# Relu-squared attention and MLP on one core: first keys in two loads, a split copy of q^T, and stores of two row positions in one

## The chip, the cores and the metric

The kernel runs on one core of one Trainium2 chip. The metric is device time in microseconds (us). The kernel before was run three times: 369.5, 369.84 and 369.86 us, a median of 369.84.

The engines are named as in the profile: PE is TensorE's matmul, PEld its weight load, DVE is VectorE, ACT is ScalarE, POOL is GpSimd and SP is SyncE. SPq, ACTq and POOLq are the queues on which these engines issue DMAs.

## What is computed

```
scores = q @ k^T / 8                     # q, k, v: 8 batches, 12 heads, 448 positions, 64 wide, float32
attn   = max(scores, 0)^2 / 448
o      = attn @ v
x      = o, heads side by side           # 3584 x 768
h      = x @ w_in                        # 768 x 2048
out    = (max(h, 0)^2) @ w_out           # 2048 x 768, out is 3584 x 768 float32
```

There is no softmax, so a score tile can be squared and used as soon as it exists.

## The kernel before

**Units and tiles.** A unit is four heads of one batch (`NU = 3` units for each of 8 batches, 24 in all). The 448 positions of a head are written as `(p j)`: 64 values of `p` and `J = 7` of `j`, so position = 7 p + j, and one partition holds 7 neighbouring positions. A unit gives 7 score tiles. Each tile is computed by `score` as 64x64 products into a PSUM slot, goes through a ReLU on ACT (line 273) into a 128x896 tile `at`, and is squared on DVE (`square0`, line 304, in the first batch; line 388 later). Then `av0` or `av_unit` multiplies it with v. There are two PSUM slots in rotation (`slot`), and a third one in the first batch (`third`).

**The head.** Units 0 to 5 are loaded as fp16 (`load16`, lines 91 to 96, POOL queue) and transposed on TensorE; units from 6 on are transposed by DMA on SP (`dma_transpose`, line 120). The order of the first batch is written out by hand in lines 804 to 898. Ten warm-up products (`warm`) run first. Then `turn_first` (lines 203 to 217) transposes q and then k of unit 0: 14 small transposes each, a copy out of PSUM, a warm-up product. DVE copies q^T whole; of k^T, ACT copies the first of 7 blocks and DVE the other six. Then come scores 0 to 3 and `pe_transpose(1)`, which turns q and k of unit 1 in one PSUM slot, with two copies on DVE (line 229). `pe_transpose(2)` comes after score 8. Argument 2 of `score`, the default of the helper `s`, runs the same products twice, which keeps TensorE busy; scores 0, 4 and 9 are run once.

**The later stages.** Two batches make a pair, pr = 0 to 3. A pair's hidden layer (line 430 for the first pair, 559 for the others) is followed by its output products (line 746), with the scores and attention products of later batches between them (`visit`).

**Output products and stores.** A row tile `(pr, tb)` is 128 rows of the pair's 896: partitions 0 to 63 are position j of one batch, 64 to 127 position j + 1, or the first position of the next batch where tb is 3. `o_groups` takes two row tiles at a time and forms seven products (`products`, lines 713 to 720) instead of eight, in two accumulators X and Y. Pairs 0 and 2 have three groups, pairs 1 and 3 have four (with row tile 6 of the pair before). The results go to `osb[0]` and `osb[1]`, 128x768 float32, of which there are two buffers each (`late["osb"]`, line 924). `end2` makes the first write of osb[0] (line 653), right after product 2; product 4 in program order (k = 3) starts afresh in the same Y. `end4` stores osb[1], `end3` stores osb[0]. A store is two DMAs on SP, one for each half of 64 partitions:

```python
b, j = divmod(2 * tb + i, J)          # i = 0, 1: the halves
out[b*S:(b+1)*S, :].rearrange("(p j) d -> p j d", j=J)[:, j, c]  <-  osb[64*i : 64*i+64, c]
```

The last group (`LAST`) stores in parts as they come: osb[0]'s first half and osb[1]'s second half on SP, osb[1]'s first half on POOL, and the rest of osb[0] in two quarters, each with one half on SP and the other on ACT.

SP's queue holds the DMA transposes and the stores in one order. Each of the 16 counters for DMAs (8 for the queues of SP and ACT, 8 for POOL) is used in rotation, so a DMA also waits for the one eight places before it.

Of the kernel before, what the change touches and what calls it, by code (L numbers as in the profile page):

```python
# [11 lines left out]
FP16 = mybir.dt.float16  # L12
FP32 = mybir.dt.float32
AF = mybir.ActivationFunctionType
# [4 lines left out]
def kernel(  # L19
# [9 lines left out]
    nc = tc.nc  # L29

    B, H, S, D = q.shape
# [11 lines left out]
    P = 128  # L43
    J = 7
# [36 lines left out]
    def heads(t, n):  # L81
        b, u = divmod(n, NU)
        return t[b].rearrange(
            "(hh u hp) (p j) d -> u (hp p) hh (j d)", hh=2, hp=2, j=J)[u]
# [6 lines left out]
    def load16(n):  # L91
        tq = q16_p.tile([P, 2, J * D], FP16, name="q16", tag="q16")
        tk = q16_p.tile([P, 2, J * D], FP16, name="k16", tag="k16")
        nc.gpsimd.dma_start(out=tq, in_=heads(q, n))
        nc.gpsimd.dma_start(out=tk, in_=heads(k, n))
        q16s[n] = (tq, tk)

    def load_v(n):
        t = v_p.tile([P, 2, J * D], FP16, name="vt", tag="vt")
        nc.gpsimd.dma_start(out=t, in_=heads(v, n))  # L100
        vts[n] = t
# [12 lines left out]
    def new_qkt():  # L114
        return [qkt_p.tile([P, J, P], FP16, name=nm, tag=nm) for nm in ("qT", "kT")]
# [30 lines left out]
    def sums_w2(i):  # L146
# [5 lines left out]
        nc.vector.tensor_sub(dst[:, c], x[:, c], y[:, c])  # L152

    load16(0)
    ident = const_p.tile([P, P], FP16, name="ident", tag="ident")
    make_identity(nc, ident)
# [37 lines left out]
    def slot(dtype, third=False):  # L194
        return (third_p if third else s_p).tile(
            [P, 2, 2048 // mybir.dt.size(dtype)], dtype, name="slot", tag="slot")

    def warm(ps, n):
        for _ in range(n):
            nc.tensor.matmul(ps[:, 0, 0:S], lhsT=zeros[:, 0:P], rhs=zeros,  # L200
                             start=True, stop=True)

    def turn_first(ps):

        ts = new_qkt()
        for i, src in enumerate(q16s.pop(0)):
            tps = slot(FP16)[:, i, 0:J * P].rearrange("p (j c) -> p j c", j=J)
            for j in range(J):
                for hh in range(2):
                    nc.tensor.transpose(  # L210
                        tps[64 * hh:64 * hh + 64, j],
                        src[:, hh, j * D:(j + 1) * D], ident)
            if i:
                nc.scalar.activation(out=ts[i][:, 0], in_=tps[:, 0], func=AF.Copy)
            nc.vector.tensor_copy(ts[i][:, i:J], tps[:, i:J])
            warm(ps, 1)
        qkt[0] = ts

    def pe_transpose(n):
        srcs = q16s.pop(n)  # L220
        ts = new_qkt()
        ps = None if n > 3 else slot(FP16)

        def copy(i, act=False):
            dst, ps = ts[i].rearrange("p j c -> p (j c)"), pss[i][:, i if n < 4 else 0, 0:J * P]
            if act:
                nc.scalar.activation(out=dst, in_=ps, func=AF.Copy)
            else:
                nc.vector.tensor_copy(dst, ps)

        if n > 3:
            pss = [mm_tile(None, FP16).rearrange("p (i c) -> p i c", i=1) for _ in range(2)]
        else:
            pss = [ps, ps]
        for i, src in enumerate(srcs):
            for j in range(J):
                for hh in range(2):
                    nc.tensor.transpose(  # L238
                        pss[i][64 * hh:64 * hh + 64, i if n < 4 else 0, j * P:(j + 1) * P],
                        src[:, hh, j * D:(j + 1) * D], ident)  # L240
        qkt[n] = ts
        if n == 3:
            return lambda: copy(0, True), lambda: copy(1)
        copy(0, n > 3)
        copy(1)
# [8 lines left out]
    def score(t, times=1, third=False, ps=None):  # L254
        n, j = divmod(t, J)
        qT, kT = qkt[n]
        spare = ps is not None
        ps = slot(FP32, third) if ps is None else [mm_tile(ps), mm_tile(ps)]
        for hh in list(range(2)) * times:
            r = slice(64 * hh, 64 * hh + 64)  # L260
            for hp in range(2):
                c = slice(64 * hp, 64 * hp + 64)
                nc.tensor.matmul(  # L263
                    ps[hh][c, 0:S] if spare else ps[c, hh, 0:S],
                    lhsT=kT[r, j, c], rhs=qT[r, :, c],
                    start=True, stop=True)
        at = at_p.tile([P, 2, S], FP16, name="at", tag="at")
        if spare:
            for hh in range(2):
                nc.scalar.activation(  # L270
                    out=at[:, hh], in_=ps[hh][:, 0:S], func=AF.Relu, scale=SK)
        else:
            nc.scalar.activation(out=at, in_=ps[:, :, 0:S], func=AF.Relu, scale=SK)  # L273
        ats[t] = at
        seen[t] = now[0]

    def av0(*tiles):

        for t in tiles:
            n, j = divmod(t, J)  # L280
            vt, at = vts[n], ats.pop(t)
            if j == 0:
                avt[0] = [p.tile([P, 512], FP32, name="avt", tag="av") for p in av_ps]
            for hp in range(2):
                r = slice(64 * hp, 64 * hp + 64)
                for hh in range(2):
                    nc.tensor.matmul(  # L287
                        avt[0][hp][64 * hh:64 * hh + 64, 0:S],
                        lhsT=vt[r, hh, j * D:(j + 1) * D], rhs=at[r, hh, :],
                        start=(j == 0), stop=(j == J - 1))  # L290
# [11 lines left out]
    def square0(*tiles):  # L302
        for t in tiles:
            nc.vector.tensor_mul(ats[t], ats[t], ats[t])  # L304
# [3 lines left out]
    def av_due(more=0):  # L308
        n = unit[0]
        return n < NUN and seen.get(n * J + J - 1, 10 ** 6) < now[0] + more  # L310
# [263 lines left out]
        return [(0.096, step(p, r, m), r == 0 and m == 0 and p not in (0, 1, 6, 8))  # L574
                for p in range(14) for r in range(2) for m in range(NH)]

    def store(row, osb, c, eng, eng2=None):
        pr, tb = row
        for i in range(2):
            b, j = divmod(2 * tb + i, J)  # L580
            b += 2 * pr
            (eng2 if eng2 and i else eng).dma_start(  # L582
                out=out[b * S:(b + 1) * S, :].rearrange(
                    "(p j) d -> p j d", j=J)[:, j, c],
                in_=osb[64 * i:64 * i + 64, c])
# [31 lines left out]
    def o_groups(groups, then):  # L617
# [5 lines left out]
        def group(n, rows, last):  # L623
# [3 lines left out]
            c0, c1 = slice(0, HALF), slice(HALF, DM)  # L627
# [8 lines left out]
            def ahead(i, k=n):  # L636
                if k < len(groups) and i not in sets[k]:
                    flush_g(needs(k))
                    sums(i, groups[k], sets[k])
# [11 lines left out]
            def plus(row, c, nm, acc=Y, cc=slice(0, HALF)):  # L651
                now_ve(0.5)
                nc.vector.scalar_tensor_tensor(  # L653
                    out=osb[row][:, c], in0=acc[0][:, 0:cc.stop - cc.start], scalar=CO,
                    in1=keep[nm][:, cc], op0=ALU.mult, op1=ALU.add)
# [8 lines left out]
            def end2():  # L664
                new_osb()
                plus(0, c0, "m1")
                if last:
                    store(rows[0], osb[0], c0, nc.sync)
# [22 lines left out]
            def end4():  # L691
                if last:
                    plus(1, c0, "u3", acc=Z)
                    store(rows[1], osb[1], c0, nc.gpsimd)
                    return
                nc.scalar.activation(out=osb[1][:, c0], in_=X[0][:, 0:HALF],
                                     func=AF.Copy, scale=CO)
                store(rows[1], osb[1], slice(0, DM), nc.sync)
                ahead(1, n + 1)
                ahead(2, n + 1)  # L700
# [5 lines left out]
            def end3_part(z):  # L706
                h = HALF // 2
                cc = slice(z * h, z * h + h)
                c = slice(HALF + cc.start, HALF + cc.stop)
                plus(0, c, "u5", acc=W, cc=cc)  # L710
                store(rows[0], osb[0], c, nc.sync, nc.scalar)

            products = (
                (X, True, lambda: tile_of(rows[0])[:, LO], b11, end1),
# [87 lines left out]
    NB0 = NU * J  # L802
    ps = slot(FP32, True)
    warm(ps, 10)
    turn_first(ps)

    def s(t, times=2):
        score(t, times, third=t in THIRD)

    THIRD = (0, 3, 5, 8, 10, 13, 16, 19)  # L810
    s(0, 1)
    s(1)
    s(2)
    s(3)
    square0(0, 1)
    pe_transpose(1)
    load16(3)
    load_w1(0)
    load_w1(1)
    load_v(3)  # L820
    s(4, 1)
    s(5)
    square0(2)
    av0(0, 1)
    s(6)
# [3 lines left out]
    square0(4)  # L829
    s(8)  # L830
    av0(3)
    square0(5, 6)
    pe_transpose(2)
    load16(4)
    load_w1(2)
    load_v(4)
    s(9, 1)
    square0(7)
    s(10)
    av0(4, 5)  # L840
    square0(8)
    s(11)
# [149 lines left out]
    for cost, fn, edge in steps:  # L992
        while ev and edge and ev[0][0] <= clock + 1e-3:
            ev.popleft()[1]()
        if edge and clock >= plan[0][0]:
# [6 lines left out]
            elif pair is not None and ahead <= 1.5 and clock > last + 1.25:  # L1002
                n = min(pair[1 + av_due(1)], NT - tile_no)
# [3 lines left out]
            elif ahead <= (1.5 if soon else 0.0) and clock > last + 1.5:  # L1007
                n = min(2, NT - tile_no)
# [38 lines left out]
```

## Time and profile before

One execution was profiled. It took 369.71 us; the profile's span is 367.9 us, and the 1.8 us left lie around it.

| stretch | us from the span's start | what ends it |
|---|---|---|
| warm-up, loads of q and k | 0 to 7.36 | k of unit 0 landed, turned and copied |
| first batch's scores | 7.36 to 27.6 | ReLU on ACT, squares and copies on DVE |
| everything up to the last products | 27.6 to 362.7 | TensorE |
| last writes and stores | 362.7 to 366.3 | landing of the last store |

The most important rows of the page, beside those shown in the prediction, are the costliest groups. L273 (ReLU) is 135.5 us of ACT, L388 (squares) 86.7 us of DVE, L746 and L559 are TensorE's output and hidden products. Idle time of an engine other than TensorE costs nothing as such. L653, the first write of an output buffer, is 30 instructions of 541 ns.

In the profile's rows, `[idle before <-releaser]` says how long the engine stood idle before the instruction and whose end let it go. The median of 52 stores of 192 KB is 3.3 us from issue to landing.

### The profile page before, as it was taken

Reading aid. Unit: us, or ns where it says so; the run is one execution under the profiler, and the core shown is the slowest. Engines: PE = TensorE matmul, PEld = TensorE weight load, DVE = VectorE, ACT = ScalarE, POOL = GpSimd, SP = SyncE. Lnnn points to the kernel's source line nnn. Section 1 sums busy time; section 2 is a strip of 40 time slices with the busy share of each in tenths; the row PEclk is TensorE's granted clock in tenths of the full one; section 3 lists DMA queues with packets and bytes.
Section 4 is the critical chain, followed back from the end, with each engine's and each line's share of the span. In section 5 each row is a group of like instructions: output and inputs, shape, how many; then the busy total and the mean of one; then the engine's idle time right before and its main releaser. Section 6 shows DMA issues by size and latency. Waiting matters only on the chain.

```text
span 367.9 us, 8740 instructions
## 1 busy us (share of the span) xinstructions
PE 358.8 (98%) x3588; PEld 232.1 (63%) x3588; DVE 265.3 (72%) x470; ACT 248.6 (68%) x384; POOL 107.2 (29%) x128
## 2 busy tenths in 40 slices
PE   8899999999999999999999999999999999999994
PEld 3644445445556788875555687886555689976662
DVE  2997677987867679888575667788876687784442
ACT  3988895788676998877655678886766785532220
POOL 8635521856552254531045225320000000000001
PEclk9999999999999999999999999999999999999999
DMA  8999999999999999967799998992323300003333
GB/s 119 196 204 203 205 204 161 144 160 166 207 124 155 170 111 134 99 92 61 138 146 125 156 159 83 107 90 52 67 71 87 86 3 2 2 0 87 86 96 78
DMA packets 121160, 42.65 MB, mean 116 GB/s; under 512 B 100832, under 2 KB 117760, under 8 KB 121120
## 3 DMA queue, kind: packets, MB, share of 16 engines
q0 software_dynamic: 82912, 23.01, 61.7%
q1 hardware_dynamic: 38048, 18.98, 26.5%
q8 instruction: 28, 0.46, 0.5%
q10 hardware_dynamic: 160, 0.10, 0.1%
q14 instruction: 12, 0.10, 0.1%
HBM read 45.61 MB, written 11.01 MB: 154 GB/s over the span
## 4 chain that ended last, share of the span: by engine, by line
PE 89%; DVE 4%; ACT 3%; issue 2%; DMA 1%; POOL 0%; POOLq 0%; ACTq 0%
PE mm L746 33%; PE mm L559 27%; PE mm L430 9%; PE slot L263 9%; PE slot L329 7%; ACT at L273 2%; DVE at L388 1%; DMA k<-in_k_dram 1%; DVE at L304 1%; PE mm L263 1%; PE avt L287 1%; PE slot L238 1%; ACT xt L342 1%; PE mm L238 0%; DVE osb L653 0%
## 5 line engine op out<-in xcount | busy, mean ns | idle before, releaser
L273 ACT ACTIVATE at<-slot 128x896 f16<-128x896 f32 x156 | 135.5, 927 | 7.4 <-PE slot L263 7.4
L388 DVE TENSOR_TENSOR at<-at 128x896 f16<-128x896 f16 x147 | 86.7, 618 | 12.6 <-ACT at L273 11.9
L109 POOL DMA_DIRECT2D qs<-in_q_dram x36 | 35.3, 983 | 111.1 <-DMA qT<-qs 102.8
L746 PEld LDWEIGHTS <-s 128*128 128x128 f16 x440 | 41.8, 98 | 32.2 <-issue 4.8
L559 PEld LDWEIGHTS <-w 128*128 128x128 f16 x576 | 53.8, 98 | 6.8 <-issue 6.0
L263 PE MATMUL slot<-qT,kT 64*64 64x448 f16 x696 | 53.2, 359 | 1.9 <-ACT at L273 1.4
L559 PE MATMUL mm<-xt,w 128*128 128x224 f16 x432 | 49.2, 259 | 0.0
L746 PEld LDWEIGHTS <-g 128*128 128x128 f16 x336 | 31.9, 98 | 23.5 <-issue 3.8
L559 PEld LDWEIGHTS <-ws 128*128 128x128 f16 x432 | 40.8, 98 | 2.8 <-issue 2.8
L746 PE MATMUL mm<-b,g 128*128 128x384 f16 x224 | 40.7, 326 | 0.0
L430 PE MATMUL mm<-xt,w 128*128 128x448 f16 x192 | 39.8, 354 | 0.0
L746 PE MATMUL mm<-b,s 128*128 128x384 f16 x216 | 39.5, 326 | 0.0
L746 PE MATMUL mm<-t,s 128*128 128x384 f16 x224 | 38.8, 326 | 0.0
L109 POOL DMA_DIRECT2D ks<-in_k_dram x36 | 35.2, 979 | 9.6 <-DMA b<-in_moe_w_out_dram 5.8
L263 PEld LDWEIGHTS <-kT 64*64 64x64 f16 x744 | 20.3, 104 | 27.6 <-issue 21.5
L653 DVE SCALAR_TENSOR_TENSOR osb<-mm,u 128x384 f32<-128x384 f32 (+1 forms) x30 | 16.2, 541 | 28.4 <-ACT u L648 20.9
L582 POOL DMA_DIRECT2D out_dram<-osb x2 | 1.1, 563 | 120.9 <-DVE osb L653 120.9
L502 DVE CUSTOM_DVE_ANT_0 g<-mm,m 128x448 f16<-128x448 f32 x36 | 22.4, 621 | 18.4 <-PE mm L559 7.8
L648 ACT ACTIVATE u<-mm 128x384 f32<-128x384 f32 x28 | 14.2, 507 | 30.5 <-PE mm L746 28.4
L559 PE MATMUL mm<-x,ws 128*128 128x224 f16 x288 | 33.7, 259 | 0.0
L329 PE MATMUL slot<-at,vt 64*64 64x448 f16 x560 | 30.1, 349 | 0.0
L430 PEld LDWEIGHTS <-w 128*128 128x128 f16 x192 | 17.1, 98 | 19.2 <-issue 5.1
(80 smaller groups left out, 417.2 us busy)
## 6 DMA issues: line engine op xcount, KB each, us to landing
out_dram<-osb SPq DMA_DIRECT2D x52, 192.0 KB, 3.3
vt<-in_v_dram POOLq DMA_DIRECT2D x24, 224.0 KB, 6.8
qs<-in_q_dram POOLq DMA_DIRECT2D x36, 112.0 KB, 4.9
ks<-in_k_dram POOLq DMA_DIRECT2D x36, 112.0 KB, 5.8
w<-in_moe_w_in_dram POOLq DMA_DIRECT2D x8, 384.0 KB, 12.1
b<-in_moe_w_out_dram POOLq DMA_DIRECT2D x4, 768.0 KB, 17.1
q<-in_q_dram POOLq DMA_DIRECT2D x6, 224.0 KB, 7.2
k<-in_k_dram POOLq DMA_DIRECT2D x6, 224.0 KB, 7.7
```

Of the source, the lines that this page charges most:

```text
L109: nc.gpsimd.dma_start(out=t[:, :, hh, :], in_=heads(src, n)[:, hh].rearrange("p (j d) -> p j d", d=D))
L238: nc.tensor.transpose(pss[i][64 * hh:64 * hh + 64, i if n < 4 else 0, j * P:(j + 1) * P], src[:, hh, j * D:(j + 1) * D], ident)
L263: nc.tensor.matmul(ps[hh][c, 0:S] if spare else ps[c, hh, 0:S], lhsT=kT[r, j, c], rhs=qT[r, :, c], start=True, stop=True)
L273: nc.scalar.activation(out=at, in_=ps[:, :, 0:S], func=AF.Relu, scale=SK)
L329: nc.tensor.matmul(ps[hp][64 * hh:64 * hh + 64, 0:S] if spare else ps[64 * hh:64 * hh + 64, hp, 0:S], lhsT=vt[r, hh, j * D:(j + 1) * D], r ...
L388: lambda: nc.vector.tensor_mul(at, at, at), 0))
L430: nc.tensor.matmul(cell[0][:, 0:S], lhsT=w1[f // 4][:, m, (f % 4) * P:(f % 4 + 1) * P], rhs=xts[b][:, m, :], start=(m == 0), stop=(m == NM ...
L502: nc.vector._custom_dve(TENSOR_ADD_SAT, out=gs(s, hi, right), in0=acc(s, y), in1=keep[s, nm], s0=3.4e38, s1=0.0)
L559: nc.tensor.matmul(XY[s][y][:, r * Q:(r + 1) * Q], lhsT=left(k, i0 + 2 * s + r, m), rhs=right(k, m), start=(fresh and r == 0 and m == 0), ...
L648: nc.scalar.activation(out=t, in_=X[0][:, 0:HALF], func=AF.Copy, scale=CO)
L653: nc.vector.scalar_tensor_tensor(out=osb[row][:, c], in0=acc[0][:, 0:cc.stop - cc.start], scalar=CO, in1=keep[nm][:, cc], op0=ALU.mult, op ...
L746: nc.tensor.matmul(acc[0][:, 0:HALF], lhsT=left()[:, f], rhs=right[:, f], start=(fresh and f == 0), stop=(f == KH - 1), skip_group_check=n ...
```

## The change

It does four things.

1. k of unit 0 is loaded in two DMAs, j = 0 to 3 and j = 4 to 6.
2. `turn_first` copies q^T with DVE (blocks 0 to 3) and ACT (4 to 6), transposes the first four blocks of k, copies block 0 and then 1 to 3 on DVE, runs score 0, and only then transposes and copies the other three blocks. q and k get a PSUM slot each, and one warm-up product of two is left out.
3. Scores 4 and 9 are placed ahead of `pe_transpose(1)` and `pe_transpose(2)`. Of the scores around them 4, 5 and 10 are run once, and 9 twice.
4. `store` writes both halves of a row tile in one DMA where both lie in the same batch (tb other than 3). In the last group osb[1]'s first half goes to ACT's queue instead of POOL's, and the two quarters go whole to ACT and to SP.

```diff
@@ load16
-        nc.gpsimd.dma_start(out=tk, in_=heads(k, n))
+        for js in (slice(0, 4), slice(4, J)) if n == 0 else (slice(0, J),):
+            c = slice(js.start * D, js.stop * D)
+            nc.gpsimd.dma_start(out=tk[:, :, c], in_=heads(k, n)[:, :, c])
@@ turn_first
-    def turn_first(ps):
-        ts = new_qkt()
-        for i, src in enumerate(q16s.pop(0)):
-            tps = slot(FP16)[:, i, 0:J * P].rearrange("p (j c) -> p j c", j=J)
-            for j in range(J):
+    def turn_first(first_score):
+        qT, kT = new_qkt()
+        qkt[0] = qT, kT
+        tq, tk = q16s.pop(0)
+        qp, kp = [slot(FP16)[:, 0, 0:J * P].rearrange("p (j c) -> p j c", j=J)
+                  for _ in range(2)]
+        def turn(dst, src, js):
+            for j in js:
                 for hh in range(2):
                     nc.tensor.transpose(
-                        tps[64 * hh:64 * hh + 64, j],
+                        dst[64 * hh:64 * hh + 64, j],
                         src[:, hh, j * D:(j + 1) * D], ident)
-            if i:
-                nc.scalar.activation(out=ts[i][:, 0], in_=tps[:, 0], func=AF.Copy)
-            nc.vector.tensor_copy(ts[i][:, i:J], tps[:, i:J])
-            warm(ps, 1)
-        qkt[0] = ts
+        turn(qp, tq, range(J))
+        nc.vector.tensor_copy(qT[:, 0:4], qp[:, 0:4])
+        nc.scalar.activation(out=qT[:, 4:J], in_=qp[:, 4:J], func=AF.Copy)
+        turn(kp, tk, range(4))
+        nc.vector.tensor_copy(kT[:, 0:1], kp[:, 0:1])
+        nc.vector.tensor_copy(kT[:, 1:4], kp[:, 1:4])
+        warm(ps, 1)
+        first_score()
+        turn(kp, tk, range(4, J))
+        nc.vector.tensor_copy(kT[:, 4:J], kp[:, 4:J])
@@ store
-    def store(row, osb, c, eng, eng2=None):
+    def store(row, osb, c, eng):
         pr, tb = row
+        b, j = divmod(2 * tb, J)
+        if j + 1 < J:
+            b += 2 * pr
+            eng.dma_start(
+                out=out[b * S:(b + 1) * S, :].rearrange(
+                    "(p j) d -> j p d", j=J)[j:j + 2, :, c],
+                in_=osb[:, c])
+            return
         for i in range(2):
             b, j = divmod(2 * tb + i, J)
             b += 2 * pr
-            (eng2 if eng2 and i else eng).dma_start(
+            eng.dma_start(
@@ end4, end3_part (last group)
-                    store(rows[1], osb[1], c0, nc.gpsimd)
+                    store(rows[1], osb[1], c0, nc.scalar)
-                store(rows[0], osb[0], c, nc.sync, nc.scalar)
+                store(rows[0], osb[0], c, (nc.scalar, nc.sync)[z])
@@ the first batch, by hand
-    turn_first(ps)
-    s(0, 1)
+    turn_first(lambda: s(0, 1))
     s(1)
     s(2)
     s(3)
+    s(4, 1)
     square0(0, 1)
     pe_transpose(1)
...
-    s(4, 1)
-    s(5)
+    s(5, 1)
...
     av0(3)
+    s(9)
     square0(5, 6)
     pe_transpose(2)
...
-    s(9, 1)
     square0(7)
-    s(10)
+    s(10, 1)
```

## The prediction

> **What bounds the kernel now.** I read the page first (busy shares, slices, the chain that ended last), then the list of DMA issues, then busy time by stage, then the timeline at the head and in the last output stage.
>
> ```profile
> span 367.9 us, 8740 instructions
> ...
> PE 358.8 (98%) x3588; PEld 232.1 (63%) x3588; DVE 265.3 (72%) x470; ACT 248.6 (68%) x384; POOL 107.2 (29%) x128
> ...
> PE   8899999999999999999999999999999999999994
> ...
> PE 89%; DVE 4%; ACT 3%; issue 2%; DMA 1%; POOL 0%; POOLq 0%; ACTq 0%
> ...
> out_dram<-osb SPq DMA_DIRECT2D x52, 192.0 KB, 3.3
> ```
>
> TensorE carries 89% of the chain and is busy in every slice but the first two and the last. So whatever delays TensorE in the middle is paid in full, and a gain can only come from the head (about 8 us) or the tail (about 5 us). Nothing in the chain is a store: each lands 3.3 us after its issue (median), far ahead of its next use.
>
> ```profile
> 93.00:120.00 27.00, 27.00 (x247) 14.88 (x246) 20.59 (x37) 18.34 (x30) 11.03 (x13) 1.00 1.27 160
> 166.00:213.00 47.00, 47.00 (x407) 26.33 (x406) 32.50 (x57) 29.07 (x48) 13.90 (x16) 1.00 0.95 128
> 257.00:293.00 36.00, 36.00 (x328) 20.52 (x327) 25.82 (x47) 24.55 (x40) 0.00 (x0) 1.00 0.31 78
> 329.00:364.00 35.00, 33.73 (x216) 20.63 (x214) 16.43 (x30) 6.87 (x14) 1.12 (x2) 1.00 0.30 82
> ```
>
> These are the stretches with stores of the four output stages (O0 to O3): window, length, PE, PEld, DVE, ACT, POOL, clock, DMA share, GB/s. PE is full in the first three. The DMA engines are crowded in O0 and O1 (the share is a sum of overlapping packet times, so it passes 1) and nearly free in O2 and O3.
>
> ```profile
> 335.96 2.48 SPq L582 DMA_DIRECT2D out_dram<-osb  x4
> 336.75 0.56 DVE L653 SCALAR_TENSOR_TENSOR osb<-mm,u 128x384 f32<-128x384 f32 x1 [1.50 <-PE mm L746]
> ...
> 345.06 2.48 SPq L582 DMA_DIRECT2D out_dram<-osb  x4
> ...
> 347.20 0.56 DVE L653 SCALAR_TENSOR_TENSOR osb<-mm,m 128x384 f32<-128x384 f32 x1 [0.80 <-PE mm L746]
> ```
>
> A group of two row tiles (9.1 us here) stores its osb1 and then, 1.4 us later, its osb0, in four issues. There are two buffers of each. So L653 at 347.20, the first write of osb0 in the third group, needs the store of the first group's osb0, issued at 337.33. It has 9.9 us; the store takes 2.8.
>
> **What the Trainium skill says.** (1) "DMA: Bandwidth & Descriptors", section "Why a DMA increments its semaphore by 16 and not by 1": a DMA runs on k of the 16 engines, k being the largest number up to 16 that divides the slowest dimension (above 1) of both access patterns; on the SP and ACT queues it takes the lowest-numbered k. (2) The same page, "Queues, rings and completion order": SP and ACT have one ring each on the same 16 engines, and each engine takes a ring in order. (3) "TensorE: Matmul & The Clock Gate", "What's actually happening": after an idle window of about 3.4 us the clock is halved until about 3.4 us of work have passed. The trace before has k = 16 only (64 rows on both sides; 16 landings for each store), so it neither supports nor contradicts (1); it agrees with (3) at the start, where full clock is granted 4.5 us after the first matmul.
>
> **The merged stores.** In the built program the DRAM side of a merged store is 2 x 64 x 768, the pair of row positions j outermost, and the SBUF side is 128 x 1 x 768. By (1) k = 2: engines 0 and 1 carry every merged store, 64 rows each, where 4 rows per engine and issue went before. 24 of the 28 row tiles are merged (not position 3, whose two halves lie in different batches). Issues fall from 62 to 35, which saves SP time that bounds nothing.
>
> Price: the trace's packet records show 121 ns for a 3072-byte packet in quiet stretches, 65 for 1536, 36 for 768. So 64 of them take S = 7.7, 4.2 and 2.3 us on one engine. Shorter is possible: packets overlap by some 16 ns in the loads (768-byte packets of 79 ns pass one in 60), and the skill's fabric ceiling (same page, "Where 436 GB/s comes from") gives an estimate of 27.2 GB/s an engine, 113 ns; with 105 ns S is 6.7. Longer is possible where loads share the engine. I take 121. The first packet comes 1.1 us after the issue, the landing 0.4 after the last packet (packet records of 361 and 359).
>
> Who waits: L653 stands on DVE and holds the sums and squares behind it. TensorE's product 3 starts afresh in the accumulator Y that this L653 reads, so TensorE follows about 0.5 us later. I write need = L653's time + 0.5.
>
> - O3 (no loads). Both engines work without a gap from 337.1: groups 1 and 2 four stores (30.8), group 3 one merged (7.7) and one unmerged (8 rows each, 1.0), the last group three half rows (12.6) and two quarters (4.6): 56.7. Last packet 393.8, landing 394.2, against 366.3 now: +27.9. On the way L653 waits: group 1's osb0 lands at 337.1 + 15.4 + 0.4 = 352.9, need 347.7; group 2's at 368.3, need 356.8 + 5.2 = 362.0. These 11.5 us lie inside the 27.9, since the engines never run dry.
> - O2. Stores of the first group at 264.93 and 267.42 land by 266.0 + 15.4 + 0.4 = 281.8; need 280.93 + 0.5: +0.5.
> - O1. First group at 175.16 and 176.81: 176.3 + 15.4 + 0.4 = 192.1, need 189.37 + 0.5: +2.2. The second group's wait behind them and behind two transposes of the same ring (1.0 each, 256-byte packets): 191.7 + 2.0 + 15.4 = 209.1, and one unit's loads lie in it (four of 0.9 and one of 1.2, the pace at which such loads land in a line: 4.8): 213.9 + 0.4. Need 201.29 + 0.5 + 2.2 = 204.0: +10.3. Together 12.5.
> - O0. Stores at 93.71 and 95.78: 94.8 + 15.4 + 0.4 = 110.6, with a unit's loads 115.4; need 108.95 + 0.5. Between 1 and 6, up to 10 if the transposes behind (97.26) come late for their scores; I take 5.
> - Cold clock: the stalls of O0 and O1 pass 3.4 us; half of 3.4 is lost in each, 3.4. The slower TensorE also gives the stores time: I take 2. In O3 it hides beneath the stores.
>
> **The head.** q landed at 5.28 and k at 6.37 (landing records), so 4/7 of k lands near 5.9. Eight transposes (14 take 0.58), then a DVE copy of 512 columns and one of 128 (625 ns for 896 and 558 for 768 give about 0.43 and 0.23; ACT's half of q^T is done by 6.6): the first score can start at 6.75 instead of 7.36. The second load adds an issue of 0.7 us on POOL in front of the identity (3.45, then 4.2; needed at 5.3) and of every later load, but the loads queue on the engines anyway (q of unit 1 is issued at 3.40 and lands at 7.90); two smaller packets cost about 0.1 us. k's rest lands at about 6.5, before the score is out of TensorE.
>
> ```profile
> 7.80 17.18 ACT L273 ACTIVATE at<-slot 128x896 f16<-128x896 f32 x21 [0.49 <-PE slot L263]
> ...
> 10.59 0.63 DVE L229 COPY qT<-slot 128x896 f16<-128x896 f16 x1 [0.40 <-PE slot L238]
> ...
> 26.40 0.62 DVE L299 TENSOR_SCALAR xt<-avt 128x448 f16<-128x448 f32 x1 [0.76 <-PE avt L287]
> 26.94 0.61 DVE L229 COPY kT<-slot 128x896 f16<-128x896 f16 x1
> 27.61 0.14 PEld L263 LDWEIGHTS <-kT 64*64 64x64 f16 x8 [0.49 <-DVE kT L229]
> ```
>
> ACT's 21 ReLUs run without a gap and move up by 0.6. DVE does not: it is nearly full from 10.59 to 25.64 (27 instructions at 0.535), and the transposes, one score later, now wait for the third ReLU (about 9.7) where they waited for the second (9.57). Its copies come 0.15 later. What is left is the 0.7 us in which DVE waited at 26.40: 0.3 of it goes. Bounds -0.6 (all that ACT gains) and +0.2 (the copies' delay); I take -0.3. The warm-up products left out (one, and one set of score 5) cover nothing that TensorE waits for.
>
> **Sum.** 27.9 + 0.5 + 12.5 + 5 + 2 - 0.3 = 47.6. The profiled execution took 369.7 (span 367.9 and 1.8 around it), 0.1 below the median: 417.3, forecast 417.
>
> **The rivals.**
> - Two engines, but only the end pays: stores are a little faster (105 ns a packet), loads yield, and O0 to O2 hide them behind the two buffers. For it: O2 is within 0.5 us of hiding already. Against it: O1's second group misses by 10. 369.7 + 27.9 - 0.3 = 397, down to 389 with faster packets.
> - Two engines, another pair each time: stores run beside one another. Group 1's osb0 in O3 lands at 337.33 + 1.1 + 7.7 + 0.4 = 346.5, before its need; the last half row on ACT at 362.25 + 1.1 + 4.2 + 0.4 = 368.0, +1.7: 371. Against it: the skill's lowest-numbered k.
> - Not slower: the store is spread over all 16 engines after all, because dimensions are reordered on the way to the queue. Its place is the tail: two issues of POOL and four quarter stores become two, the last quarter lands near 363.15 + 2.1 (the smallest landing time shown) + 0.3 instead of 366.3, about -0.7, and with the head -0.3: 368.7. It decides as soon as k is 8 or more: S is then at most 1.9 us and no buffer is late. Against it: nothing in the built program shows a reordering.
>
> **Chances.** Forecast's mechanism in all stages 0.72, with its own range 398 (105 ns) to 440 (loads and transposes late too). Only the end 0.12 (388 to 398), changing pair 0.05 (371), sixteen engines 0.11 (368.7). 0.2% is 0.74 us, about what a measurement of this kernel can tell from no change. Of the last case 0.07 is faster by more, 0.04 within; all others are slower. The range 388 to 445 takes in the first two cases but for their edges, about 0.8.
>
> **What would show it.** Right: stores that land 10 to 20 us after issue; L653 (L675 after) waiting for DMA out_dram in O1 and O3; PE gaps there; SP's landings as the end of the chain, with TensorE done some 15 us earlier; in the head, the first score near 6.8. Wrong: stores landing in 3 us, or a span below 375, would say that k is not 2 on fixed engines; a first score after 7.2, that half of k does not land early.

## The result and the profile after

| | before | after |
|---|---|---|
| device time, median | 369.85 us (4 runs, 369.5 to 370.1) | 439.44 us (4 runs, 437.47 to 441.23) |
| span of the profiled execution | 367.9 us | 435.9 us |
| mean granted TensorE clock | 0.999 | 0.937 |

The change makes the kernel slower by 19%: the ratio is 1.188, with a 95% interval of 1.181 to 1.195. The forecast was 417, with a range of 388 to 445. The four runs of the changed kernel lie in two pairs, at 437.5 to 437.7 and at 441.2, so two or three us between single runs of kernels like it decide nothing.

In the code after, L653 has become L675, L746 is L768, L559 is L572, L263 is L276; L596 issues the merged stores, L604 those that still go in halves. These are the lines of its page that answer to those shown of before: busy time, TensorE in 40 slices, its granted clock, the queue that carries instructions (packets, MB, share), the chain by engine and by line, two groups of instructions, and the list of DMA issues.

```profile
span 435.9 us, 8694 instructions
PE 372.5 (85%) x3583; PEld 237.0 (54%) x3583; DVE 264.9 (61%) x472; ACT 249.7 (57%) x384; POOL 105.8 (24%) x127
PE   7999999999599919999757989399999999967630
...
PEclk9999999999799988999997999789999999997785
...
q8 instruction: 28, 0.46, 0.5%
...
PE 60%; DMA 25%; DVE 4%; issue 3%; ACT 2%; POOL 1%; SPq 0%; DVEq 0%; ACTq 0%; POOLq 0%
PE mm L572 23%; DMA out_dram<-osb 21%; PE mm L768 16%; PE mm L443 8%; PE slot L276 6%; PE slot L342 5%; DMA kT<-ks 2%; ACT at L286 2%; DMA vt<-in_v_dram 1%; DVE osb L675 1%; DVE at L401 1%; DVE at L317 1%; PE avt L300 1%; PE slot L251 0%; DVE s L637 0%
...
L111 POOL DMA_DIRECT2D qs<-in_q_dram x36 | 35.1, 977 | 158.8 <-DMA qT<-qs 152.6
...
L675 DVE SCALAR_TENSOR_TENSOR osb<-mm,m 128x384 f32<-128x384 f32 x14 | 7.8, 557 | 44.1 <-DMA out_dram<-osb 37.2
...
out_dram<-osb SPq DMA_DIRECT2D x22, 384.0 KB
```

The chain was 89% TensorE and 1% DMA; now a quarter of it is DMA, and 21% is stores. L675, the first write of an output buffer, waits 37.2 us in all for stores, where before it never waited for one. But two further things stand out that stores alone don't explain: the transposed keys (`kT<-ks`) are on the chain, and the granted clock is below full speed in several slices.

To see where the 68 us arise, cut both executions at the same place in the work, the issue of the first store of each output stage O0 to O3. The windows view of before, and then of after (window, length, busy time and count of PE, PEld, DVE, ACT, POOL, clock, DMA share, GB/s):

```profile
93.71:175.16 81.45, 81.45 (x854) 56.12 (x852) 65.15 (x119) 63.28 (x98) 31.22 (x34) 1.00 1.16 127
175.16:264.93 89.77, 89.77 (x906) 61.47 (x904) 65.28 (x118) 64.94 (x104) 23.98 (x26) 1.00 0.85 113
264.93:335.96 71.03, 71.03 (x694) 52.85 (x693) 51.65 (x93) 41.88 (x69) 0.00 (x0) 1.00 0.13 35
```

```profile
93.84:193.41 99.57, 85.99 (x854) 57.97 (x852) 65.53 (x119) 63.51 (x98) 31.03 (x34) 0.93 1.44 104
193.41:304.77 111.36, 93.82 (x906) 63.07 (x904) 64.97 (x118) 65.37 (x104) 23.72 (x26) 0.94 1.29 91
304.77:376.39 71.62, 71.05 (x694) 52.85 (x693) 51.22 (x93) 41.90 (x69) 0.00 (x0) 1.00 0.10 34
```

The counts of PE agree row by row (854, 906, 694), so it is the same work. O0's stretch is longer by 18.1 us, O1's by 21.6, O2's by 0.6. In the first two TensorE is busy 4.5 and 4.1 us longer with the same products: that is the lower clock (worked out below). The rest, 13.6 and 17.5 us, it stands idle. From O3's first store to the end it is 58.1 us (376.39 to the last landing at 434.49) against 30.4: 27.7 more. Up to O0's first store the two differ by 0.13 us.

The idle time has few places. The timeline of TensorE after, all gaps of more than 1 us between 94 and 376 (start, length, instruction, and in brackets the idle time and what ended it):

```profile
115.99 2.72 PE L768 MATMUL mm<-t,s 128*128 128x384 f16 x8 [4.85 <-DVE osb L675]
...
162.97 0.59 PE L276 MATMUL slot<-qT,kT 64*64 64x448 f16 x4 [8.73 <-DMA kT<-ks]
...
212.06 1.46 PE L768 MATMUL mm<-t,s 128*128 128x384 f16 x8 [2.44 <-DVE osb L675]
...
231.35 2.72 PE L768 MATMUL mm<-t,s 128*128 128x384 f16 x8 [7.29 <-DVE osb L675]
...
253.90 0.46 PE L572 MATMUL mm<-x,ws 128*128 128x224 f16 x3 [1.24 <-issue]
...
274.36 0.56 PE L276 MATMUL slot<-qT,kT 64*64 64x448 f16 x6
281.49 0.58 PE L276 MATMUL slot<-qT,kT 64*64 64x448 f16 x2 [6.57 <-issue]
```

Three are the waits that the prediction names: product 3 behind L675 behind a store, 4.85 + 2.44 + 7.29 = 14.6 us. The gap of 8.73 us is a score that waits for transposed keys: by the landing records they landed at 162.93, and TensorE went on at 162.97.

The other two, 1.24 + 6.57 = 7.8 us, bear only the word issue: in the trace the instruction after each waits for nothing. They are not waits for transposes. At 253.90 TensorE goes on with hidden products in the middle of a group of twelve, and at 281.49 with the last two of eight score products, six of which had run at 274.36. Each stop ended 0.3 to 0.4 us after a transpose of queries had landed (253.62 and 281.12), but the scores of that unit need its keys as well, and these landed at 255.44 and 282.52, after TensorE had gone on.

What the two stops share is their place in TensorE's program. The page's queue q8 carries instructions in 28 packets, each of 16384 bytes in the packet records, and the trace holds 7196 records of TensorE, 257 for each packet. TensorE stopped after 4545 and after 5057 of them: 512, or twice 256, apart, and 449 beyond 16 and 18 times 256. The 17th and the 19th packet, at 250.09 and 278.93, began when TensorE stood 398 and 449 records beyond these multiples. All others from the sixth on, counted in the same way, began at 157 to 299, and in the kernel before at 157 to 280. So it seems that TensorE had used up its instructions because a packet was late; why it went on only 2.5 and 1.6 us after the two packets' ends (251.36 and 279.92) is not known. The run below with merged stores in all but the last stage stops after 5057 records too, for 4.68 us; the kernel before has no such stop. No run was made to test this reading.

Why are transposes late? Two of SP's issues in O0 before, and then its queue after:

```profile
97.26 1.49 SPq L120 DMA_TRANSPOSE qT<-qs  x1
98.86 2.66 SPq L120 DMA_TRANSPOSE kT<-ks  x1
```

```profile
93.84 2.58 SPq L596 DMA_DIRECT2D out_dram<-osb  x2
96.71 13.26 SPq L122 DMA_TRANSPOSE qT<-qs  x1
110.07 3.17 SPq L122 DMA_TRANSPOSE kT<-ks  x1
113.34 1.96 SPq L604 DMA_DIRECT2D out_dram<-osb  x2
115.39 0.54 SPq L596 DMA_DIRECT2D out_dram<-osb  x1
116.10 8.59 SPq L122 DMA_TRANSPOSE qT<-qs  x1
124.79 3.45 SPq L122 DMA_TRANSPOSE kT<-ks  x1
128.35 3.68 SPq L596 DMA_DIRECT2D out_dram<-osb  x2
```

The second column is how long SP held the instruction. The first transpose behind stores is held 8.6 to 15.3 us in O0, the second 3.2 to 3.5, where each took 1.4 to 2.9 us before. What stands behind it on SP is late as well: the stores of 113.34 were issued at 106.40 before. And as these transposes empty the buffers `qs` and `ks`, POOL's next loads wait too (152.6 us in the page's row of L111, against 102.8 before).

The landing records say how a merged store travels. The one issued at 93.84 shows three events: one at 95.02, then 106.13 and 106.16. The early one comes long before the data can have passed; the other two are the only engines that report an end. A store in halves shows 16 landings. In quiet O3 the two engines hand over one store every 7.53 us (landings 386.79, 394.32 and 401.86 of three stores in a row), 118 ns for each of 64 rows.

### The profile page after: what moved, and what is told of

The parts are those of the page before. It is cut to its first block, busy times and chain, and to the rows that moved or that the text cites. A ratio compares the mean times of both kernels' runs of the same rounds, so it can differ in the third digit from the quotient of the medians.

```text
span 435.9 us, 8694 instructions
## 1 busy us (share of the span) xinstructions
PE 372.5 (85%) x3583; PEld 237.0 (54%) x3583; DVE 264.9 (61%) x472; ACT 249.7 (57%) x384; POOL 105.8 (24%) x127
## 4 chain that ended last, share of the span: by engine, by line
PE 60%; DMA 25%; DVE 4%; issue 3%; ACT 2%; POOL 1%; SPq 0%; DVEq 0%; ACTq 0%; POOLq 0%
PE mm L572 23%; DMA out_dram<-osb 21%; PE mm L768 16%; PE mm L443 8%; PE slot L276 6%; PE slot L342 5%; DMA kT<-ks 2%; ACT at L286 2%; DMA vt<-in_v_dram 1%; DVE osb L675 1%; DVE at L401 1%; DVE at L317 1%; PE avt L300 1%; PE slot L251 0%; DVE s L637 0%
## 5 line engine op out<-in xcount | busy, mean ns | idle before, releaser
L768 PEld LDWEIGHTS <-s 128*128 128x128 f16 x440 | 44.3, 103 | 63.3 <-issue 38.7
L111 POOL DMA_DIRECT2D qs<-in_q_dram x36 | 35.1, 977 | 158.8 <-DMA qT<-qs 152.6
L276 PE MATMUL slot<-qT,kT 64*64 64x448 f16 x692 | 53.9, 361 | 16.5 <-DMA kT<-ks 8.7
L768 PE MATMUL mm<-t,s 128*128 128x384 f16 x224 | 44.8, 354 | 25.6 <-DVE osb L675 25.6
L572 PEld LDWEIGHTS <-w 128*128 128x128 f16 x576 | 55.1, 100 | 7.8 <-issue 6.4
L572 PE MATMUL mm<-xt,w 128*128 128x224 f16 x432 | 51.4, 266 | 0.0
L768 PEld LDWEIGHTS <-g 128*128 128x128 f16 x336 | 32.0, 98 | 23.8 <-issue 4.1
L572 PEld LDWEIGHTS <-ws 128*128 128x128 f16 x432 | 41.6, 100 | 4.8 <-issue 4.3
L276 PEld LDWEIGHTS <-kT 64*64 64x64 f16 x740 | 20.6, 104 | 42.4 <-issue 27.4
L768 PE MATMUL mm<-b,s 128*128 128x384 f16 x216 | 42.8, 344 | 0.0
L768 PE MATMUL mm<-b,g 128*128 128x384 f16 x224 | 40.7, 326 | 0.0
L111 POOL DMA_DIRECT2D ks<-in_k_dram x36 | 34.6, 965 | 14.0 <-DMA kT<-ks 6.6
L572 PE MATMUL mm<-x,ws 128*128 128x224 f16 x288 | 35.2, 266 | 1.2 <-issue 1.2
L675 DVE SCALAR_TENSOR_TENSOR osb<-mm,u 128x384 f32<-128x384 f32 (+1 forms) x30 | 16.2, 543 | 32.7 <-ACT u L670 25.2
L675 DVE SCALAR_TENSOR_TENSOR osb<-mm,m 128x384 f32<-128x384 f32 x14 | 7.8, 557 | 44.1 <-DMA out_dram<-osb 37.2
L521 DVE TENSOR_TENSOR g<-g 128x896 f16<-128x896 f16 x48 | 28.8, 620 | 0.4 <-ACT g L524 0.4
```

What stands on the lines that cost most here:

```text
L111: nc.gpsimd.dma_start(out=t[:, :, hh, :], in_=heads(src, n)[:, hh].rearrange("p (j d) -> p j d", d=D))
L276: nc.tensor.matmul(ps[hh][c, 0:S] if spare else ps[c, hh, 0:S], lhsT=kT[r, j, c], rhs=qT[r, :, c], start=True, stop=True)
L521: lambda: nc.vector.tensor_mul(g, g, g), b))
L572: nc.tensor.matmul(XY[s][y][:, r * Q:(r + 1) * Q], lhsT=left(k, i0 + 2 * s + r, m), rhs=right(k, m), start=(fresh and r == 0 and m == 0), ...
L675: nc.vector.scalar_tensor_tensor(out=osb[row][:, c], in0=acc[0][:, 0:cc.stop - cc.start], scalar=CO, in1=keep[nm][:, cc], op0=ALU.mult, op ...
L768: nc.tensor.matmul(acc[0][:, 0:HALF], lhsT=left()[:, f], rhs=right[:, f], start=(fresh and f == 0), stop=(f == KH - 1), skip_group_check=n ...
```

## Experiments

**The last stage alone, and all but the last stage.** Is the loss of a stage its own?

```diff
-        if j + 1 < J:
+        if j + 1 < J and pr == 3:    # e3_only_o3; pr < 3 in e4_not_o3
```

> The changed kernel with merged stores in the last pair alone (O3); the other three output stages store in two halves as before. Theory (the stage sum of the prediction holds for O3: two engines write without a gap to the end): O0 to O2 as before, O3 from first store to last landing about 58 us instead of 30.4, time 369.8 + 27.7 = 397.5 (396.5 to 398.5). Rival (O3 is long only because earlier stages leave work or a low clock behind): O3 below 50 us, time below 390.

> The changed kernel with merged stores in pairs 0 to 2 alone. Theory (the stages add up; O0 costs about 18 us, O1 about 21.5, O2 under 1): the first store of O3 is issued near 376.4 us, O3 takes about 30.4 us, the time is 369.8 + 40.5 = 410 (408 to 413). Rival (a stage's loss is partly taken back by the next, or passed on to it): the time is more than 3 us off 410.

Measured beside 369.69 of before, in one run each: 396.11 for O3 alone (+26.4), 412.38 for the others (+42.7). The sum, 69.1, meets the whole change's 69.6 more closely than single runs can show. In the first, O3 took 56.3 us from first store to last landing (336.24 to 392.54); the time came out 0.4 us below the expected band. In the second, O3 took 30.6 (378.60 to 409.21); it began 2.2 us later than in the changed kernel, and the trace has 37.6 us of half clock ahead of it, against 27.3 there. Within two or three us the stages add up: neither passes a loss on nor takes one back.

**Transposes on another queue.** The changed kernel, and as a control the kernel with stores in halves, each with the transposes issued by ACT. This asks whether the place behind the stores in SP's queue is what makes the transposes late.

```diff
-            nc.sync.dma_start_transpose(
+            nc.scalar.dma_start_transpose(
```

> The changed kernel, all stores merged, with the DMA transposes of q and k issued on ACT's queue instead of SP's. Theory (on SP's queue a transpose stands behind merged stores: its issue takes 8 to 15 us, and loads, scores and later stores wait for that): issues of transposes fall to 1.2 to 2 us, TensorE no longer waits for kT, the first store of O1 comes at most 8 us later than before (183 or less instead of 193.4), the time falls by 10 to 20 us to 420 to 430. Rival (the queue does not matter, the transposes need the same two engines, which are taken): transposes land as late as now, O1 starts after 190, the time stays within 5 us of 439, or rises if ACT stands in the issue.

> Control for the run before: stores in two halves on SP as before, transposes on ACT's queue. If ACT has room for 38 issues of about 1.3 us beside its work (it is busy for 68% of the span): 369.8 to 373. If the issues delay ReLUs: each of some 38 issues costs up to 1.3 us, up to 420; what it takes above 370 is to be taken off the run before.

Measured: 480.04 and 423.75 us, one run each. ACT has no room for these issues: the control alone loses 54 us, more than its expectation allowed for. Taken off as that expectation says, this leaves 426, inside the expected 420 to 430; but two losses in one kernel need not add up, so the times decide nothing about the cause. The landing records say more, since they can be read transpose by transpose in O0 (issue to last landing, us):

| transposes in O0 | before, SP | after, SP | merged, ACT | halves, ACT |
|---|---|---|---|---|
| behind stores | 6.5 to 9.1 | 9.9 to 24.0 | 13.0 to 16.8 | 2.9 to 4.6 |

(For the third column the first pair, 3.7 and 3.3 us, is left out: it was issued before any store.) The issues on ACT's queue, merged stores:

```profile
111.24 1.24 ACTq L122 DMA_TRANSPOSE qT<-qs  x1
112.59 5.97 ACTq L122 DMA_TRANSPOSE kT<-ks  x1
...
129.71 1.78 ACTq L122 DMA_TRANSPOSE qT<-qs  x1
131.66 5.92 ACTq L122 DMA_TRANSPOSE kT<-ks  x1
...
151.79 1.24 ACTq L122 DMA_TRANSPOSE qT<-qs  x1
153.14 6.31 ACTq L122 DMA_TRANSPOSE kT<-ks  x1
```

The first transpose of a pair, which was held 8.6 to 15.3 us on SP, is now held 1.2 to 1.8; the second is held longer, 5.9 to 6.3 instead of 3.2 to 3.5. So most of the long hold is of SP's own queue. But a landing still takes 13 us and more, against 3 to 5 with stores in halves. Both theories hold in part. From the issue of a pair's first transpose to the landing of its second it is 22.2 to 25.3 us in the changed kernel, 15.0 to 18.1 with merged stores on ACT, and 4.6 to 5.4 with halves on ACT: the queue adds some 7 us, the merged stores on the DMA engines some 10 to 13. As the pace of these kernels is another one, these are sizes, not exact prices.

That a transpose has to wait its turn on the two engines of the stores fits the packet records, but is argued, since they do not name the engine. From 116 to 126 us in the third column's run the transposes passed 94 to 141 packets of 256 bytes in each us, about 6 to 9 for each of sixteen engines, while the merged stores passed 13 to 16 packets, 7 or 8 for each of two; without a store beside them, from 99 to 101 us, the transposes passed 562 and 904. The sixteen landings of each of these transposes lie within 1.8 us, so it ends on all engines nearly together.

**The rest of the change, without its stores.**

> All of the change but the stores: parts 1 to 3 stay, stores go in two halves and the last group on the queues of before. The prediction's term for the head: 369.85 - 0.3 = 369.5 (ratio 0.9992). What the changed kernel's trace shows (first output store 0.13 us later than before): 369.85 + 0.1 = 370.0 (1.0003). Rival (the head has a cost that the trace of one execution hides): above 370.6.

The edit is the change with `store` and the last group's queues as before. Measured: 369.93 against 369.76 us, ratio 1.0003, interval 0.9995 to 1.0012. The forecast's -0.3 us (0.9992) lies outside it; +0.1 fits. O0's first store was issued at 93.85, 0.14 later than before.

**The same merging on sixteen engines.** A merged store needs its rows in one dimension. If the columns of a batch's tiles stand in the order of positions, a row tile is 128 neighbouring rows of the output, and its store has 128 outermost on both sides. Bytes, queues and number of DMAs stay those of the change, but for tile 3, which is merged too. The first way was to let the ReLU write in that order:

```diff
+        r = 2 * pr * S + tb * P
+        eng.dma_start(out=out[r:r + P, c], in_=osb[:, c])
...
-            nc.scalar.activation(out=at, in_=ps[:, :, 0:S], func=AF.Relu, scale=SK)
+            nc.scalar.activation(
+                out=at.rearrange("p h (c j) -> p h j c", j=J),
+                in_=ps[:, :, 0:S].rearrange("p h (j c) -> p h j c", j=J),
+                func=AF.Relu, scale=SK)
```

> The changed kernel with one DMA for each row tile, 384 KB as in the change, but 128 rows in a row of the output and in the row of partitions on both sides: the ReLU of the scores writes its columns in the order of positions, so that a row tile is 128 neighbouring rows of the output (tile 3 is merged too). Theory (what costs is that the outermost dimension of the merged store is 2, so that two engines carry it): 16 landings per store, 2.5 to 5 us from issue to landing, no wait for a store, time 369 to 370.5. Rival (the size of one DMA, or one DMA in place of two, costs): above 385. A strided write of the ReLU that is slower than 0.82 us would show in the head and in ACT's busy time, and adds up to 21 times the difference.

> The kernel before, its head included, with the stores of the run above (one DMA of 128 neighbouring rows, last group on SP and ACT alone). If the tail's share of the prediction's third rival holds (-0.7 us from fewer issues at the end): 369.15, ratio 0.998. If the stores at the end are bounded by what DVE hands out: 369.85.

> As the run two above, but each row tile in two DMAs of 116 and 12 neighbouring rows: 116 = 4 x 29, so by the divisor rule four engines carry 29 rows each. Theory: four landings for each DMA of 116 rows, 29 x 0.117 + 1.5 = 4.9 us from issue to landing in O3, no wait of L675, the tail at most 3 us later than with 16 engines: 370 to 376. Rival (the engines' number is set by something else than a divisor of the rows, such as the bytes): 16 landings, time as with 128 rows.

Measured: 804.05, 804.29 and 814.61 us, all three spoilt by one thing. The group of the ReLU in the first:

```profile
L288 ACT ACTIVATE at<-slot 128x896 f16<-128x896 f32 x156 | 561.1, 3812 | 4.5 <-PE slot L276 4.5
```

It takes 3812 ns where it took 927: a write to SBUF with a step of 14 bytes costs four times a write in a row, and ACT becomes the bound. The expectation named that risk, but as a small one. As instruments for the time these runs failed; their stores are still readable. Those of 128 rows show 16 landings, all within 2.34 us of the issue in O3. In the third run a store of 116 rows (4 x 29) shows four landings after the early one, one of 12 rows shows twelve.

**The order changed where it is cheap.** Only the copies of x out of PSUM are changed, and the step is put on the side that is read:

```diff
-            out=xts[b][:, 2 * u:2 * u + 2, :], in_=ps[:, :, 0:S],
+            out=xts[b][:, 2 * u:2 * u + 2, :].rearrange("p h (c j) -> p h c j", j=J),
+            in_=ps[:, :, 0:S].rearrange("p h (j c) -> p h c j", j=J),
```

> The question of the run with 128 neighbouring rows again, with the change of order put where it touches 24 instructions instead of 180: the copies of x out of PSUM (917 ns for 128x896 on ACT before) read PSUM with a step of 64 elements and write SBUF in a row; the ReLUs are as in the change. Stores: one DMA of 384 KB for each row tile, 128 rows outermost on both sides. Theory (two engines are the whole cost of the merged stores): 16 landings, 2.3 us each as in that run, no wait for a store, no late transpose; if a copy of x keeps its 0.92 us, 369.3 to 370.5; if reading with a step costs as much as writing with one did (4.6 times), 24 copies of 3.3 us more, up to 79 us, most of it on TensorE's path. Rival (merging as such costs): O3 from first store to end over 35 us.

Measured: 368.86 against 369.62 us, ratio 0.9983, interval 0.9974 to 0.9992: the whole loss is gone, and the kernel is a little faster than before. From the page's groups and DMA issues:

```profile
L357 ACT ACTIVATE xt<-slot 128x896 f16<-128x896 f32 x20 | 18.3, 917 | 7.6 <-PE slot L343 7.5
...
out_dram<-osb SPq DMA_DIRECT2D x26, 384.0 KB, 2.5
```

The copy takes 917 ns, as before the change. The store of 384 KB lands 2.5 us after its issue (median), where two of 192 KB each took 3.3. No instruction waits for a store in this kernel's table of waits. So what costs in the change is the number of engines, not the size or the number of DMAs. The rows of a store now also lie side by side in the output, but that is not it: before, on sixteen engines with rows seven apart, stores landed 2.7 to 3.1 us after their issue in O3 (the smaller pieces of the last group sooner).

**Four engines.**

```diff
-        eng.dma_start(out=out[r:r + P, c], in_=osb[:, c])
+        for a, e in ((0, 116), (116, P)):
+            eng.dma_start(out=out[r + a:r + e, c], in_=osb[a:e, c])
```

> The run with one DMA of 128 neighbouring rows and the change of order in the copies of x, but each row tile in two DMAs of 116 and 12 rows. By the divisor rule 116 = 4 x 29 goes over four engines, 12 over twelve. Theory: four landings for a store of 116 rows, 5 to 8 us from issue to landing in O3, the two buffers of osb cover it for the most part, the last store lands 1 to 4 us later: 370 to 385. With two engines it was 439.4 and with sixteen 368.9, so a loss in proportion to the time that the busiest engine needs per tile (64, 29 and 8 rows) would give 368.9 + 70.5 x 21 / 56 = 395; a value far below that says that the loss begins only where the store outlasts its buffer.

Measured: 378.92 us (two runs, 377.22 and 380.61), ratio 1.024, interval 1.020 to 1.029. One wait for a store is left, and it is short (us in all, times, longest):

```profile
DVE osb L666 <- DMA out_dram<-osb: 0.9, 1, 0.9
```

The first store of O3 is issued at 336.32, 0.4 us later than with sixteen engines, so O0 to O2 hide the slower stores almost whole; the last landing is 8.5 us later (373.65 against 365.14). At the end the stores pile up, and the last two issues, at 369.24 and 369.44, each wait for the DMA eight places before it (the one issued at 358.29 landed at 369.22). The tail is worth more than the 1 to 4 us expected. The proportional rival (395) falls. This run also has two DMAs for each row tile, so not all of its loss need be of the engines.

**The tail, and the best version.** Where does the gain over before come from?

> The kernel before, with the last group's stores on the queues of the change (osb1's first half on ACT, one quarter of osb0 whole on ACT, the other whole on SP), each still in two DMAs of 64 rows. The prediction's third rival put the tail at -0.7 us: 369.1 (ratio 0.998). If the last quarter's two issues on one queue cost as much as they save: 369.8 to 370.2.

> The kernel before, with its own head, with one DMA of 128 neighbouring rows for each row tile, the change of order in the copies of x, and the last group's stores on SP and ACT alone. If the gain of the run with the changed head (368.86) is all of the tail (there the last landing is 1.2 us earlier, at 365.14 instead of 366.32): 368.5 to 368.9, the same as with the changed head within 0.2%. If the changed head has a part in it: 369.3 or more.

New queues for the last group with stores still in halves: 369.88 against 369.62, ratio 1.001 (1.0004 to 1.0017), a trifle slower; four issues of ACT now stand in a row (2.93 us from 362.17). The old head with whole-tile stores: **368.30** against 369.69 us, ratio 0.9962, interval 0.9951 to 0.9974, 0.2 us below its expected band and the fastest version of the study. The landing records of the last store in each:

| kernel | issue | last landing | us |
|---|---|---|---|
| before (second half, on ACT) | 363.44 | 366.32 | 2.88 |
| changed head, 128 rows a store | 363.09 | 365.14 | 2.05 |
| old head, 128 rows a store | 362.97 | 364.89 | 1.92 |

As the queues alone bring nothing, one issue in place of two at the very end is worth some 1.2 to 1.4 us. Between the last two the head shows again: O0's first store is at 93.66 with the changed head and 93.53 with the old one, 0.13 apart, as in the earlier pair. The times differ by more, 0.56 us, and they were not taken side by side.

## Why the prediction was right, and where it was short

The mechanism of the forecast, two fixed engines under every merged store, is what happened. The Trainium skill, page "DMA: Bandwidth & Descriptors", section "Why a DMA increments its semaphore by 16 and not by 1", gave the rule before any trace had it; the runs agree, with 2, 4, 12 and 16 landings for outermost dimensions of 2, 116, 12 and 64 or 128. Its early write of the remainder fits the event about 1 us after the issue (0.4 on four engines). The three rivals fall: 397 (only the end pays) because O0 and O1 do lose 40 us; 371 (changing pair) because stores follow one another every 7.53 us; 368.7 (all sixteen) because only two engines report. That last figure is met by 368.86 once the rows are put in one dimension, but by other terms: some 1.2 us in the tail where 0.7 was put down, and a head that loses 0.1 instead of gaining 0.3. That it fits is luck.

The range took in the result, but the sum covers only 47.6 of the 69.6 us. The chances name 440 for "loads and transposes late too", which is where the result lies; no sum stood behind that figure.

| term of the forecast's sum | forecast, us | measured, us |
|---|---|---|
| O3 | 27.9 | 27.7 |
| O2 | 0.5 | 0.6 |
| O1, waits for output buffers | 12.5 | 9.7 (2.44 + 7.29) |
| O0, wait for an output buffer | 5 | 4.9 |
| score that waits for a transpose, O0 | none set | 8.7 |
| TensorE stops, it seems for instructions, O1 | none set | 7.8 (1.24 + 6.57) |
| cold clock | 2 | 8.6 (4.54 + 4.05) |
| head, up to O0's first store | -0.3 | +0.1 |
| sum | 47.6 | 68.1 |

For O2 the forecast's own numbers give 281.8 - 281.43 = 0.4, where it wrote 0.5.

- **O3 was right in its parts.** S was put at 7.7 us and measured 7.53. L675 waits where foretold, 7.62 and 5.64 us, for the first and the second group's osb0 (5.2 and 6.3 were put down). TensorE's last product ends 16 us before the last landing (418.1 and 434.49).
- **The transfers beside the stores were left at nothing.** The forecast priced what transposes do to stores ("behind two transposes of the same ring (1.0 each, 256-byte packets)") and not what stores do to transposes. It came near once: O0 "up to 10 if the transposes behind (97.26) come late for their scores; I take 5". The 5 was spent on the buffer. It took the landing of a transpose as given; this went from 6.5 to 9.1 us to 9.9 to 24.0 in O0, SP's queue was held up to 15 us, and a score stood still for 8.73. In O1 the transposes behind stores landed 6.3 to 26.7 us after their issue, yet no stop of TensorE there is shown to be theirs. There it was, by all that the trace shows, TensorE's own instructions that came late, 7.8 us, of which the forecast does not speak.
- **The cold clock was mis-sized.** "The stalls of O0 and O1 pass 3.4 us; half of 3.4 is lost in each, 3.4", of which 2 was taken. With the two long stops that were not foreseen (8.73 and 6.57) there are four stretches at half clock ahead of O3 in the trace's clock records, each 6.83 us long (from 114.98, 159.35, 227.62 and 278.82). TensorE works 5.8, 3.2, 3.1 and 4.2 us in them, and half of that, 8.1 us, is near the 8.6 by which its busy time grew.
- **The head's sign was wrong**, by 0.4 us. The timeline of after shows why the first score came at 7.02 and not at 6.75:

```profile
6.02 0.42 DVE L222 COPY qT<-slot 128x512 f16<-128x512 f16 x1 [4.92 <-PE slot L217]
...
6.47 0.49 ACT L223 ACTIVATE qT<-slot 128x384 f16<-128x384 f16 x1 [4.23 <-DVE qT L222]
...
7.02 0.38 PE L276 MATMUL slot<-qT,kT 64*64 64x448 f16 x4 [0.46 <-ACT qT L223]
...
7.45 4.96 ACT L286 ACTIVATE at<-slot 128x896 f16<-128x896 f32 x6 [0.48 <-PE slot L276]
...
11.04 0.62 DVE L242 COPY qT<-slot 128x896 f16<-128x896 f16 x1 [1.21 <-PE slot L251]
```

The two copies of q^T were meant to run side by side; ACT's began only when DVE's had ended, 0.4 us later than its input was there. In the trace's record it waits on the semaphore that DVE's copy sets, so the wait stands in the program. The ReLUs gain 0.35 us all the same (7.45 against 7.80). But the transposes' copies on DVE come at 11.04 instead of 10.59, three times the delay that was put down, and DVE sets the end of the first batch. That reading of the head was not tested part by part: its effect is too small for that.

What stays open: how the lateness of a transpose divides between SP's queue and the engines' share, exactly, and whether TensorE's two stops in O1 are late instructions, as their place in the program says. More output buffers, which would take the waits of L675 away and leave the rest, were not tried.

## What to carry to other kernels

Before merging two DMAs, look at the outermost dimension of both access patterns: a pair dimension of 2 in front sends everything through two engines, and the cure is to arrange the data so that the long dimension stands first. When a transfer gets slow, price it in both directions: what waits for it, and what stands behind it on its queue and on its engines, such as transposes and loads with due times of their own, and perhaps the program itself. If an order of elements has to change, put the step on a PSUM read of the smallest set of instructions, not on an SBUF write.

## What the runs showed of the hardware that was not expected

- **Step on the write against step on the read.** ACT writing fp16 to SBUF with a step of 14 bytes: 3812 ns for 128x896 instead of 927. ACT reading float32 from PSUM with a step of 256 bytes and writing in a row: 917 ns, no change.
- **A transpose holds its queue.** SP held a transpose for up to 15.3 us behind two merged stores; a merged store behind another was held 2.5 us at most in O0.
- **Two and four engines kept one pace per row, but four started slowly.** In quiet O3, two engines took 7.53 us for 64 rows of 3072 bytes each, 118 ns a row. On four engines the first two stores of 116 rows landed 3.54 to 3.58 us apart on each engine; with one row of the store of 12 rows between them that is 30 rows, 118 to 119 ns each. But the first of the two landed 7.54 us after its issue, 4.0 us more than these rows take, where two engines needed 2.9 more (10.41) and sixteen 1.4 (2.32 for 8 rows each). In its first us some packets took 1.2 to 1.4 us instead of 121 ns. Why was not followed up.
- **Half clock came in multiples of 3.41 us.** In the changed kernel's trace, six stretches before TensorE's last product are 6.83 us long; each began 2.6 to 5.1 us into an idle gap of 4.24 to 8.73 us. A gap of 2.44 us brought none; in the run with merged stores in all but the last stage, however, one of 2.43 us brought 3.41 us of half clock, and one of 12.90 us brought 13.65.
- **TensorE's program came by DMA, a packet for some 257 of its records.** Two packets that began late, after 398 and 449 records instead of 157 to 299, go with two stops of TensorE that nothing else in the trace explains.
